# A second block of weights converted behind the attention's first stage, and half of the next layer's weights inside that layer's loop

## The chip, the cores and the metric

The kernel runs on one core of a Trainium2 chip. The metric is the device time of one execution in microseconds (us), the median of several runs. Five engines matter: PE (TensorE, the matrix multiplier), DVE (VectorE), ACT (ScalarE), POOL (GpSimd) and SP (SyncE, which here only issues DMA transfers). Each works through its own list of instructions in the order in which the program puts them there.

## The reference

Three stages follow one another: a causal attention with a bias from a running sum, a feed-forward layer with a PReLU, and one with a gate by a clipped sum. Cut to what matters:

```python
# attention: 4 batches x 8 heads x 576 positions x 64
scores = q @ k.T / sqrt(64)
cum = cumsum(maximum(s, 0))
scores = where(causal, -1e6 or lower, scores + minimum(-(cum_row - cum_col), 0))
attn = exp(scores - max); attn = attn / (sum(attn) + 1e-9)
x = attn @ v                                   # 2304 tokens x 512
# layer one: 512 -> 2048 -> 512
h = x @ w_in;  g = maximum(h, 0) + alpha * minimum(h, 0);  y = g @ w_out
# layer two: 512 -> 2048 -> 512
h = y @ w_in2; g = h * clip(h + 3, 0, 6) / 6;              out = g @ w_out2
```

The weights come as 64-bit floats.

## The kernel before, in words

**Precision.** Every product of the two layers is three matmuls: each operand is split into a high and a low part of a 32-bit type (`fp32r`), and high by low, low by high and high by high are added up. A matmul works on a 128x128 weight and up to 512 columns.

**Weights.** A layer's weights are read as pairs of 32-bit words and converted on the chip. They come in eight units; a unit serves two of the sixteen steps `f` of the layer's hidden dimension. `load_unit` issues its four transfers on SP (tiles `wraw`, 512 KB each), and `split_unit` converts it in two parts, each with one tile of the first matrix (`wi`) and one of the second (`wo`). `split_part` (L128 to L159) is one part: ACT takes the upper words over into a buffer `wcv` (L141, per tile), POOL clamps that (L143) and writes a copy back (L146), ACT prepares the lower words of `wi` (L149; only outside the attention's first stage), DVE puts the words together (L151, and L154 where L149 did not run), ACT rounds to the high part (L157) and DVE subtracts for the low part (L158). So a unit is 10 instructions on DVE outside the first stage and 12 for a unit whose buffers belong to it, 8 on POOL, and 8 to 10 on ACT. `wi` of both parts is needed for step `f`'s first product, since a part is half of the contraction.

**Stages.** The first stage (L633 to L636) is the attention of the first 256 tokens of each batch for the heads of batches 0 and 1 (eight pairs of heads): scores (PE L242), bias and maximum on DVE (L234, L247), a mask on POOL (L236), exponentials on ACT (L251), scaling on POOL (L255), transposes on PE (L486) and values (L493, L494), whose result ACT and DVE split into `xhi` (L498) and `xlo` (L499). The second stage (L637 to L672) runs layer one for those tokens (blocks 0 and 1, 512 columns at a time) with the heads of batch 2 and more between its steps. `moe1` (L544) is layer one: step `f` makes `h` (PE, helper `products`, L181; 12 matmuls), `gt` on ACT and DVE (L581, L582), `gh` (ACT L585) and `gl` (DVE or POOL, L586), and some steps later the second product `y` (PE L559; 12 matmuls). After the second stage come the rest of the attention with layer one for blocks 3 and on, then a last call of layer one for the last two blocks (L698 to L704), which also converts the second weights (`more_w2`), and layer two (L710 to L762): `h` (PE L749), `gt` (ACT L751, DVE L752), `gh` and `gl` (ACT L755, DVE L756) and `o` (PE L722, L725), with the next block's input fetched at step 4 (`load_y`, L688: a transfer, ACT L694, DVE L695).

**What sets the order.** The program's own scheduler orders each engine's list by priorities; `tc.high_priority(offset=...)` shifts them. `more_w` converts the first weights' next unit: inside the first stage with the offset `WP0`, which puts the work behind other work; `W_AT` names the heads at which `attend` calls it there. `tc.keep_in_program_order` ties an instruction to a place behind the one that the program wrote before it on the same engine. Conversion buffers `wcv` lie in the stage's pool (`Pools`), six of them in the first stage; a later stage's buffers take the same memory and wait until it is free.

Of the kernel before, what the change touches and what calls it, by code (L numbers as in the profile page):

```python
# [22 lines left out]
WB0 = 6  # L23
WB = 4

W_LD = (8, 11, 14)
W_AT = (2, 14)

A2_AT = 2
A2_OF = 11  # L30
# [10 lines left out]
W_SCALE = 2.0**-112  # L41
W_MOST = struct.unpack("f", struct.pack("I", 0x0FEFFFFF))[0]
# [16 lines left out]
def attention_moe_moe(ctx, tc, qt, kt, qn, kn, vp, s, w_in1, w_out1, alpha, w_in2, w_out2, out):  # L59

    nc = tc.nc
# [8 lines left out]
    NU = 8  # L70
# [22 lines left out]
    def bank(role):  # L93
        turn[role] = turn.get(role, -1) + 1
        i = roles[role][turn[role] % len(roles[role])]
        return ps.tile([P, 512], F32, tag=f"b{i}", name=role)
# [28 lines left out]
                raw[nm, part] = t  # L125
        return j, raw

    def split_part(unit, part, pool, tag, bufs):  # L128
        j, raw = unit
        names = [("wi", part), ("wo", part)]  # L130
        ops = []
        for key in names:
            c = pool.tile([P, CH], U32, tag=tag, bufs=bufs, name="wcv")
            r = raw[key]
            half = r.bitcast(U16).rearrange("p f (t b) -> p f t b", t=2)

            beside = (half[:, :, 1, 0], half[:, :, 0, 1]) if bufs != WB0 and key[0] == "wi" else None
            ops.append((c, c.bitcast(F32), r[:, :, 1], r[:, :, 0], beside))

        for c, cf, high, low, beside in ops:  # L140
            nc.scalar.activation(cf, high.bitcast(F32), AF.Copy, scale=W_SCALE)  # L141
        for c, cf, high, low, beside in ops:
            nc.gpsimd.tensor_scalar(cf, cf, W_MOST, -W_MOST, op0=ALU.min, op1=ALU.max)  # L143

        for c, cf, high, low, beside in ops:
            nc.gpsimd.tensor_scalar(high.bitcast(F32), cf, 0.0, 1.0, op0=ALU.mult, op1=ALU.mult)  # L146
        for c, cf, high, low, beside in ops:
            if beside:
                nc.scalar.activation(*beside, AF.Copy, scale=1.0 / 8192, bias=-4095.5 / 8192)  # L149
        for c, cf, high, low, beside in ops:  # L150
            nc.vector.scalar_tensor_tensor(c, c, 3, high, op0=ALU.logical_shift_left, op1=ALU.bitwise_or)  # L151
        for c, cf, high, low, beside in ops:
            if not beside:
                nc.vector.scalar_tensor_tensor(c, low, 29, c, op0=ALU.logical_shift_right, op1=ALU.bitwise_or)  # L154
        for key, (c, cf, *_) in zip(names, ops):
            t = wp.tile([P, 2, CH], F32R, tag=f"{key[0]}{j}{part}", name=key[0])
            nc.scalar.activation(t[:, 0, :], cf, AF.Copy)  # L157
            nc.vector.tensor_tensor(t[:, 1, :], cf, t[:, 0, :].bitcast(F32), op=ALU.subtract)  # L158
            raw[key] = t  # L159

    def split_unit(unit, pool, tag, bufs):
        for part in range(NP):
            split_part(unit, part, pool, tag, bufs)
        return unit[1]

    def w_in_of(w, kc, f):
# [428 lines left out]
    units, w1, units2, w2 = [], [], [], []  # L595

    def load_w1(n):
        while len(units) < n:
            units.append(load_unit(w_in1, w_out1, len(units)))

    def more_w(pool):
        if len(w1) < NU:
            load_w1(len(w1) + 1)
            with tc.high_priority(offset=WP0 if pool.wb == WB0 else 0):
                w1.append(split_unit(units[len(w1)], pool, "wcv", pool.wb))

    def more_w2(f, pool):

        if f >= 2 and f % 2 == 0 and len(units2) < NU:
            units2.append(load_unit(w_in2, w_out2, len(units2)))  # L610
        if f >= 6 and f % 2 == 0 and len(w2) < NU:
            with tc.high_priority(offset=W2P):
                w2.append(split_unit(units2[len(w2)], pool, "wcv", pool.wb))

# [59 lines left out]
    with ExitStack() as st:  # L674
        pool = Pools(st, tc, "attb", ("kraw qraw vraw ks qh ql vs cum", "t", "xf pth ptl"))
# [22 lines left out]
    with ExitStack() as st:  # L698
        pool = Pools(st, tc, "last", ("g5 gh5 gl5 wcv",), WB)
# [10 lines left out]
    with ExitStack() as ph2:  # L710
        m2 = Pools(ph2, tc, "moe2", ("y", "g gh gl ot", "wcv"))
# [86 lines left out]
```

## Time and profile before

| | us |
|---|---|
| median of 3 runs | 1040.13 (1039.94 to 1040.81) |
| the profiled execution, whole | 1040.27 |
| its span (first to last instruction) | 1038.5 |
| PE busy | 1012.4 (97%) |
| DVE busy | 622.5 (60%) |
| ACT busy | 567.9 (55%) |
| POOL busy | 432.6 (42%) |

The page of the profile gives each engine's busy time and the chain of work that ended last. The timeline lists instructions in order of time: start and length in us, the engine, the line of the program, the operation, the tiles (output, arrow, inputs), and how many equal ones were merged; in brackets stands how long the engine was idle ahead of it and what released it. Starts count from the beginning of the span. The view by stretches gives for each stretch the busy time of every engine, the clock that PE was granted as a share of its upper level of 2.4 GHz, and the load of the DMA engines. The view by lines groups instructions.

### The profile page before, as it was taken

The numbers are of one execution on the slowest core, as the hardware profiler recorded it, in microseconds if no ns is written. First come the engines' busy times: TensorE is split into PE (matmuls) and PEld (weight loads), VectorE is DVE, ScalarE is ACT, GpSimd is POOL, SyncE is SP. The second block draws the span as 40 slices with busy tenths as digits, with TensorE's granted clock in tenths as the row PEclk, the third lists the DMA queues.
The fourth block names the chain that finished last, engine by engine and source line by source line (L and its number), as shares of the span: only waits on it lengthen the run. The fifth ranks groups of instructions, "written<-read, shape, count | busy, mean of one in ns | idle before, by whom it ended". The sixth has DMA issues, their size and how long they took to land.

```text
span 1038.5 us, 17002 instructions
## 1 busy us (share of the span) xinstructions
PE 1012.4 (97%) x5843; PEld 868.1 (84%) x5843; DVE 622.5 (60%) x1520; ACT 567.9 (55%) x1286; POOL 432.6 (42%) x625
## 2 busy tenths in 40 slices
PE   7899999999999999999999998999999999999998
PEld 3457777999999999999998886888888888888897
DVE  4849995668888888888854999623222322222222
ACT  3557885767776767777745788523222422322232
POOL 4836763957877778877731664200000000000000
PEclk6799999999999999999999999999999999999999
DMA  6829004413334233334206653100100100000010
GB/s 205 307 75 351 12 16 116 144 46 110 94 92 122 82 98 111 100 97 113 69 8 209 238 187 132 66 1 9 73 1 1 61 1 0 21 21 1 1 41 21
DMA packets 55893, 89.59 MB, mean 86 GB/s; under 512 B 5568, under 2 KB 29888, under 8 KB 55808
## 3 DMA queue, kind: packets, MB, share of 16 engines
q1 hardware_dynamic: 55808, 88.52, 27.2%
q8 instruction: 46, 0.75, 0.3%
q14 instruction: 39, 0.32, 0.1%
HBM read 78.99 MB, written 9.51 MB: 85 GB/s over the span
## 4 chain that ended last, share of the span: by engine, by line
PE 88%; DVE 3%; ACT 3%; DMA 2%; issue 1%; POOL 1%; SPq 1%; ACTq 0%; POOLq 0%; DVEq 0%
PE h L749 18%; PE h L181 18%; PE y L559 18%; PE o L722 13%; PE o L725 6%; PE s L319 4%; PE pv L381 4%; PE pt L356 4%; PE s L242 1%; DMA wraw<-in_w_in 1%; PE pt L486 1%; PE pv L493 1%; ACT wcv L141 1%; ACT t L251 0%; DVE wcv L154 0%
## 5 line engine op out<-in xcount | busy, mean ns | idle before, releaser
L181 PE MATMUL h<-xhi,wi 128*128 128x256 f32 (+1 forms) x896 | 221.2, 317 | 1.6 <-DVE gt L582 1.5
L749 PE MATMUL h<-yhl,wi 128*128 128x512 f32 (+1 forms) x960 | 213.6, 371 | 4.1 <-DVE gt L752 4.1
L749 PEld LDWEIGHTS h<-yhl,wi 128*128 128x128 f32 x960 | 170.4, 189 | 37.6 <-DVE gt L752 4.5
L752 DVE SCALAR_TENSOR_TENSOR gt<-gt,h 128x512 f32<-128x512 f32 (+1 forms) x80 | 50.6, 634 | 211.6 <-ACT gt L751 211.3
L181 PEld LDWEIGHTS h<-xhi,wi 128*128 128x128 f32 x896 | 154.6, 189 | 15.7 <-DVE gt L582 2.6
L559 PE MATMUL y<-gh,wo 128*128 128x256 f32 (+1 forms) x896 | 162.3, 316 | 0.0
L751 ACT ACTIVATE gt<-h,three 128x512 f32<-128x512 f32 (+1 forms) x80 | 51.4, 645 | 200.4 <-PE h L749 199.6
L722 PE MATMUL o<-wo,gh 128*128 128x512 f32 x576 | 145.7, 391 | 0.1
L559 PEld LDWEIGHTS y<-gh,wo 128*128 128x128 f32 x896 | 132.7, 190 | 11.6 <-issue 1.3
L181 PE MATMUL h<-xlo,wi 128*128 128x256 f32 (+1 forms) x448 | 141.4, 316 | 0.0
L722 PEld LDWEIGHTS o<-wo,gh 128*128 128x128 f32 x576 | 106.8, 188 | 22.7 <-ACT gh L755 0.6
L559 PE MATMUL y<-gl,wo 128*128 128x256 f32 (+1 forms) x448 | 93.8, 317 | 0.0
L181 PEld LDWEIGHTS h<-xlo,wi 128*128 128x128 f32 x448 | 84.8, 189 | 6.0 <-issue 0.2
L327 ACT ACTIVATE t<-t,m 128x384 f32<-128x384 f32 (+2 forms) x96 | 67.5, 703 | 40.6 <-DVE m L322 39.5
L143 POOL TENSOR_SCALAR wcv<-wcv 128x512 f32<-128x512 f32 x64 | 52.0, 817 | 88.1 <-ACT wcv L141 85.0
L756 DVE TENSOR_TENSOR gl<-gt,gh 128x512 fp32r<-128x512 f32 (+1 forms) x80 | 51.2, 641 | 55.5 <-ACT gh L755 45.8
L331 POOL TENSOR_SCALAR t<-t,rec 128x384 f32<-128x384 f32 (+2 forms) x96 | 67.6, 705 | 30.7 <-DVE rec L330 22.3
L725 PE MATMUL o<-wo,gl 128*128 128x512 f32 x288 | 79.4, 390 | 0.0
L755 ACT ACTIVATE gh<-gt 128x512 fp32r<-128x512 f32 (+1 forms) x80 | 47.1, 588 | 56.0 <-DVE gt L752 41.1
L582 DVE SCALAR_TENSOR_TENSOR gt<-gt,beta,h 128x256 f32<-128x256 f32 (+1 forms) x112 | 61.4, 549 | 26.2 <-ACT gt L581 25.5
L559 PEld LDWEIGHTS y<-gl,wo 128*128 128x128 f32 x448 | 70.8, 190 | 5.9 <-issue 0.3
L586 POOL TENSOR_TENSOR gl<-gt,gh 128x256 fp32r<-128x256 f32 x80 | 63.1, 788 | 29.8 <-ACT gh L585 29.7
(101 smaller groups left out, 1787.4 us busy)
## 6 DMA issues: line engine op xcount, KB each, us to landing
wraw<-in_w_in SPq DMA_DIRECT2D x32, 512.0 KB, 5.4
wraw<-in_w_out SPq DMA_DIRECT2D x32, 512.0 KB, 5.7
kraw<-in_kt SPq DMA_DIRECT2D x32, 288.0 KB, 2.8
cumk<-cum_scratch SPq DMA_DIRECT2D x32, 288.0 KB, 3.3
qraw<-in_qt SPq DMA_DIRECT2D x32, 160.0 KB, 2.7
vraw<-in_vp SPq DMA_DIRECT2D x32, 160.0 KB, 2.2
y_scratch<-yt SPq DMA_DIRECT2D x18, 256.0 KB, 3.0
yr<-y_scratch SPq DMA_DIRECT2D x4, 1024.0 KB, 5.2
```

The lines of the kernel that those rows point to most:

```text
L143: nc.gpsimd.tensor_scalar(cf, cf, W_MOST, -W_MOST, op0=ALU.min, op1=ALU.max)
L181: nc.tensor.matmul(dst, lt, r, start=first and i == 0, stop=last and i == len(terms) - 1)
L327: nc.scalar.activation(t[:n, :w], t[:n, :w], AF.Exp, bias=m[-1][:n], scale=-1.0, accum_out=den[:n])
L331: nc.gpsimd.tensor_scalar(t[:n, :w], t[:n, :w], rec[:n], 1.0, op0=ALU.mult, op1=ALU.mult)
L559: nc.tensor.matmul(ys[dc // per][:, o : o + n], which[:, dc * P : (dc + 1) * P], gg, start=(f == 0 and which is wl and dc % per == 0), sto ...
L582: nc.vector.scalar_tensor_tensor(gt, gt, beta[:, f : f + 1], hp[:, :n], op0=ALU.mult, op1=ALU.add)
L586: (nc.vector if n == 512 else nc.gpsimd).tensor_tensor(gl, gt, gh.bitcast(F32), op=ALU.subtract)
L722: nc.tensor.matmul(op[i], lt[:, tsl], r, start=(f == 0 and r is wh), stop=False)
L725: nc.tensor.matmul(op[i], gl[:, tsl], wh, start=False, stop=(f == FC - 1))
L749: nc.tensor.matmul(hp[:, :n], lt, r, start=(i == 0), stop=(i == len(terms) - 1))
L751: nc.scalar.activation(gt[:, :n], hp[:, :n], AF.Relu, bias=three)
L756: nc.vector.tensor_tensor(gl[:, :n], gt[:, :n], gh[:, :n].bitcast(F32), op=ALU.subtract)
```

## The change

Four edits:

- `W_AT` goes from (2, 14) to (2, 17): the first weights' second unit (unit 1, for steps 2 and 3) is converted when the program's loop over the first stage's heads is over, not at head 14. Its instructions get the new `pin`, by which each keeps its place behind the instruction that the program wrote before it on its engine.
- The first stage's pools are set up in another order, so that the conversion buffers `wcv` lie last.
- `more_w2` stops at four units (`NU // 2`) in place of eight. Before, six units were written in that last call of layer one, and two more in layer two's loop.
- Layer two's loop writes the other four units (4 to 7), with `pin`, at its steps 4, 6, 8 and 10 of the first block.

```diff
-W_AT = (2, 14)
+W_AT = (2, 17)
...
-    def split_part(unit, part, pool, tag, bufs):
+    def split_part(unit, part, pool, tag, bufs, pin=False):
+        keep = tc.keep_in_program_order if pin else (lambda ins: ins)
...
-            nc.scalar.activation(cf, high.bitcast(F32), AF.Copy, scale=W_SCALE)
+            keep(nc.scalar.activation(cf, high.bitcast(F32), AF.Copy, scale=W_SCALE))
...
-                w1.append(split_unit(units[len(w1)], pool, "wcv", pool.wb))
+                w1.append(split_unit(units[len(w1)], pool, "wcv", pool.wb, pin=len(w1) == 1))
...
-        if f >= 6 and f % 2 == 0 and len(w2) < NU:
+        if f >= 6 and f % 2 == 0 and len(w2) < NU // 2:
...
-        pool = Pools(st, tc, "att0", ("wcv", "kraw qraw vraw cum", "t pT"), WB0)
+        pool = Pools(st, tc, "att0", ("kraw qraw vraw cum", "t pT", "wcv"), WB0)
...
-                    w2.append(split_unit(units2[len(w2)], m2, "wcv", 3))
+                    w2.append(split_unit(units2[len(w2)], m2, "wcv", 3, pin=True))
```

`keep` goes around each of the eight instructions of `split_part` in the same way. Lines from 129 on stand two lower in the kernel after (L149 is L151 there, L582 is L584).

The names in the rows below: `h_886` and `h_942` belong to steps 0 and 1, `h_1082` and `h_1118` to steps 2 and 3, `h_1220` to step 4; `wcv_802`, `803`, `820`, `821` with `wi_814`, `wo_817`, `wi_832`, `wo_835` are unit 1 in the kernel after; `wcv_850` to `869` are unit 2 and `906` to `925` unit 3; `t_982` and `s_988` are the second stage's first head.

DVE, at the end of the first stage, before: behind the last `xlo` come the gates of steps 0 and 1, between them the bias of the second stage's first heads, and unit 2's conversion.

```order
L499 TENSOR_TENSOR xlo_82<-pv_831,xhi_81 128x256
L582 SCALAR_TENSOR_TENSOR gt_899<-gt_899,beta_79,h_886 128x512
L234 TENSOR_SCALAR t_982<-cumk_969,cq_83 128x128
L234 TENSOR_SCALAR t_982<-cumk_969,cq_83 128x256
L582 SCALAR_TENSOR_TENSOR gt_955<-gt_955,beta_79,h_942 128x512
L234 TENSOR_SCALAR t_1002<-cumk_969,cq_83 128x128
L234 TENSOR_SCALAR t_1002<-cumk_969,cq_83 128x256
L586 TENSOR_TENSOR gl_903<-gt_899,gh_902 128x512
L586 TENSOR_TENSOR gl_959<-gt_955,gh_958 128x512
...
L151 SCALAR_TENSOR_TENSOR wcv_850<-wcv_850,wraw_597 128x512
L151 SCALAR_TENSOR_TENSOR wcv_851<-wcv_851,wraw_599 128x512
```

After, the same place: the gates, then the conversion of units 2, 1 and 3, 32 instructions (`wcv_850` to `wo_835`), of which the sixteenth is unit 1's `wi_814` and the last two are `wi_832` and `wo_835`; only then step 2's gate and the first head.

```order
L501 TENSOR_TENSOR xlo_82<-pv_795,xhi_81 128x256
L584 SCALAR_TENSOR_TENSOR gt_899<-gt_899,beta_79,h_886 128x512
L584 SCALAR_TENSOR_TENSOR gt_955<-gt_955,beta_79,h_942 128x512
L588 TENSOR_TENSOR gl_903<-gt_899,gh_902 128x512
L588 TENSOR_TENSOR gl_959<-gt_955,gh_958 128x512
L153 SCALAR_TENSOR_TENSOR wcv_850<-wcv_850,wraw_597 128x512
...
L160 TENSOR_TENSOR wi_814<-wcv_802,wi_814 128x512
...
L160 TENSOR_TENSOR wo_939<-wcv_925,wo_939 128x512
L160 TENSOR_TENSOR wi_832<-wcv_820,wi_832 128x512
L160 TENSOR_TENSOR wo_835<-wcv_821,wo_835 128x512
L584 SCALAR_TENSOR_TENSOR gt_1095<-gt_1095,beta_79,h_1082 128x512
L236 TENSOR_SCALAR t_982<-cumk_969,cq_83 128x128
```

The conversion of three units has moved ahead of the second stage's first head, in one piece.

PE, at the same place, before: the last matmuls of steps 0 and 1, the scores of the first head, and the matmuls of step 2, whose weights (`wi_733`, `wi_751`, unit 1 of that kernel) were converted in the first stage.

```order
L181 MATMUL h_886<-xhi_81,wi_251 128x512
L181 MATMUL h_942<-xlo_82,wi_251 128x512
L181 MATMUL h_942<-xhi_81,wi_251 128x512
L242 MATMUL s_988<-kraw_962,qraw_964 128x128
L242 MATMUL s_988<-kraw_962,qraw_964 128x256
L181 MATMUL h_1082<-xhi_81,wi_733 128x512
L181 MATMUL h_1082<-xlo_82,wi_733 128x512
L181 MATMUL h_1082<-xhi_81,wi_733 128x512 x2
L181 MATMUL h_1082<-xlo_82,wi_733 128x512
L181 MATMUL h_1082<-xhi_81,wi_733 128x512
L181 MATMUL h_1082<-xhi_81,wi_751 128x512
L181 MATMUL h_1082<-xlo_82,wi_751 128x512
```

After: behind steps 0 and 1 come their second products `y` (24 matmuls, of which the last stands first here), 12 matmuls of steps 2 and 3 on `wi_814`, 12 on `wi_832`, and then the first head's scores and step 4 on unit 2 (`wi_862`).

```order
L561 MATMUL y_1105<-gl_959,wo_254 128x512
L183 MATMUL h_1082<-xhi_81,wi_814 128x512
...
L183 MATMUL h_1118<-xhi_81,wi_814 128x512
L183 MATMUL h_1082<-xhi_81,wi_832 128x512
L183 MATMUL h_1082<-xlo_82,wi_832 128x512
...
L183 MATMUL h_1118<-xhi_81,wi_832 128x512
L244 MATMUL s_988<-kraw_962,qraw_964 128x128
L244 MATMUL s_988<-kraw_962,qraw_964 128x256
L183 MATMUL h_1220<-xhi_81,wi_862 128x512
L183 MATMUL h_1220<-xlo_82,wi_862 128x512
```

The scores of the second stage's first head have moved from behind 24 matmuls of layer one to behind 72.

DVE, at the start of layer two, before: conversion stands right ahead of the first two gates of layer two (`gt2`).

```order
L154 SCALAR_TENSOR_TENSOR wcv_9324<-wraw_9095,wcv_9324 128x512
L154 SCALAR_TENSOR_TENSOR wcv_9631<-wraw_9203,wcv_9631 128x512
L158 TENSOR_TENSOR wi_9642<-wcv_9630,wi_9642 128x512
L158 TENSOR_TENSOR wo_9338<-wcv_9324,wo_9338 128x512
L158 TENSOR_TENSOR wo_9645<-wcv_9631,wo_9645 128x512
L752 SCALAR_TENSOR_TENSOR gt2_9366<-gt2_9366,h_9353 128x512
L752 SCALAR_TENSOR_TENSOR gt2_9386<-gt2_9386,h_9373 128x512
```

After: the last call of layer one's gates stand there, and the first conversion (`wcv_9401`, unit 4) comes behind the gates of four more steps.

```order
L584 SCALAR_TENSOR_TENSOR gt_9218<-gt_9218,beta_79,h_9205 128x512
L588 TENSOR_TENSOR gl_9222<-gt_9218,gh_9221 128x512
L754 SCALAR_TENSOR_TENSOR gt2_9294<-gt2_9294,h_9281 128x512
L697 TENSOR_TENSOR yhl_9471<-yr_9469,yhl_9471 128x512 x4
...
L754 SCALAR_TENSOR_TENSOR gt2_9450<-gt2_9450,h_9437 128x512
L758 TENSOR_TENSOR gl2_9454<-gt2_9450,gh2_9453 128x512
L153 SCALAR_TENSOR_TENSOR wcv_9401<-wcv_9401,wraw_8981 128x512
L153 SCALAR_TENSOR_TENSOR wcv_9402<-wcv_9402,wraw_8983 128x512
L156 SCALAR_TENSOR_TENSOR wcv_9402<-wraw_8983,wcv_9402 128x512
L160 TENSOR_TENSOR wi_9413<-wcv_9401,wi_9413 128x512
```

The conversions ahead of layer two's first gates have gone, and four units now stand between its steps.

## Rows read from the trace of the kernel before

**Rows 1.** The page, busy time by engine.

```profile
PE 1012.4 (97%) x5843; PEld 868.1 (84%) x5843; DVE 622.5 (60%) x1520; ACT 567.9 (55%) x1286; POOL 432.6 (42%) x625
```

**Rows 2.** Timeline of ACT, DVE and PE around the end of stage one.

```profile
73.72 0.39 ACT L498 ACTIVATE xhi<-pv 128x256 fp32r<-128x256 f32 x1 [4.46 <-PE pv L494]
74.00 2.32 ACT L141 ACTIVATE wcv<-wraw 128x512 f32<-128x512 f32 x4
76.22 1.07 ACT L581 ACTIVATE gt<-h 128x512 f32<-128x512 f32 x2
77.62 0.63 ACT L585 ACTIVATE gh<-gt 128x512 fp32r<-128x512 f32 x1 [0.33 <-DVE gt L582]
...
79.57 1.49 DVE L586 TENSOR_TENSOR gl<-gt,gh 128x512 fp32r<-128x512 f32 x2
...
88.66 0.61 PE L559 MATMUL y<-gh,wo 128*128 128x512 f32 x2
```

**Rows 3.** View by lines, 74 to 160 us: busy, mean ns of one, idle before.

```profile
L151 DVE SCALAR_TENSOR_TENSOR wcv<-wcv,wraw 128x512 uint32<-128x512 uint32 x24 | 18.5, 778 | 3.0 <-ACT wraw L149 2.8
L158 DVE TENSOR_TENSOR wi<-wcv,wi 128x512 fp32r<-128x512 f32 x12 | 11.0, 919 | 0.7 <-ACT wi L157 0.7
L158 DVE TENSOR_TENSOR wo<-wcv,wo 128x512 fp32r<-128x512 f32 x12 | 9.9, 828 | 1.6 <-ACT wo L157 1.4
L154 DVE SCALAR_TENSOR_TENSOR wcv<-wraw,wcv 128x512 uint32<-128x512 uint32 x12 | 9.5, 793 | 0.0
...
L149 ACT ACTIVATE wraw<-wraw 128x512 uint16<-128x512 uint16 x12 | 16.3, 1357 | 0.0
L141 ACT ACTIVATE wcv<-wraw 128x512 f32<-128x512 f32 x24 | 15.9, 675 | 3.3 <-DVE wi L158 1.7 <-DVE wo L158 1.5
...
L157 ACT ACTIVATE wi<-wcv 128x512 fp32r<-128x512 f32 x12 | 7.6, 634 | 1.4 <-DVE wcv L151 1.4
```

**Rows 4.** Timeline of DVE ahead of layer two's first gates.

```profile
638.16 1.28 DVE L151 SCALAR_TENSOR_TENSOR wcv<-wcv,wraw 128x512 uint32<-128x512 uint32 x2
...
646.30 1.28 DVE L752 SCALAR_TENSOR_TENSOR gt<-gt,h 128x512 f32<-128x512 f32 x2
```

**Rows 5.** Stretches: length, busy of PE, PEld, DVE, ACT, POOL; PE clock, DMA.

```profile
156.00:182.00 26.00, 25.08 (x141) 20.84 (x140) 14.49 (x38) 13.93 (x37) 10.26 (x17) 1.00 0.41 118
182.00:208.00 26.00, 24.40 (x199) 23.54 (x198) 16.70 (x58) 19.82 (x65) 25.11 (x41) 1.00 0.47 141
...
638.00:646.00 8.00, 4.98 (x22) 3.76 (x20) 7.90 (x14) 7.37 (x13) 0.00 (x0) 1.00 0.49 160
```

**Rows 6.** PE at layer two's start (timeline); twelve matmuls at full clock (chain).

```profile
647.03 7.36 PE L749 MATMUL h<-yhl,wi 128*128 128x512 f32 x24 [4.05 <-DVE gt L752]
...
99.53 2.72 PE y L559 x12
```

**Rows 7.** Issues on SP (timeline); landing of weight loads, 70 to 130 us.

```profile
73.75 0.80 SPq L476 DMA_DIRECT2D cumk<-cum_scratch  x2
...
77.44 0.43 SPq L123 DMA_DIRECT2D wraw<-in_w_in  x1
...
DMA to landing us min/median/max: 7.0/9.3/10.5
```

**Rows 8.** Stage one: PE (timeline), clock (stretches), unit 1's first DVE step.

```profile
35.74 0.92 PE L242 MATMUL s<-kraw,qraw 64*128 64x128 f32 x4 [1.58 <-DVE m L247]
38.68 1.65 PE L242 MATMUL s<-kraw,qraw 64*128 64x128 f32 x4 [2.02 <-DVE m L247]
...
60.57 1.15 PE L486 MATMUL pt<-ident,t 128*128 128x128 f32 x3 [1.17 <-POOL t L255]
...
48.00:50.00 2.00, 1.92 (x6) 1.20 (x7) 2.00 (x5) 0.66 (x2) 2.00 (x3) 0.50 0.71 252
...
62.00:64.00 2.00, 2.00 (x8) 1.08 (x7) 0.00 (x1) 0.80 (x2) 2.00 (x6) 0.50 0.00 0
...
44.63 0.68 DVE L151 SCALAR_TENSOR_TENSOR wcv<-wcv,wraw 128x512 uint32<-128x512 uint32 x1
```

More of the change, by code (lines that the diff above doesn't have):

```diff
@@ L140, in split_part, with split_unit @@
         for c, cf, high, low, beside in ops:
-            nc.scalar.activation(cf, high.bitcast(F32), AF.Copy, scale=W_SCALE)
+            keep(nc.scalar.activation(cf, high.bitcast(F32), AF.Copy, scale=W_SCALE))
         for c, cf, high, low, beside in ops:
-            nc.gpsimd.tensor_scalar(cf, cf, W_MOST, -W_MOST, op0=ALU.min, op1=ALU.max)
+            keep(nc.gpsimd.tensor_scalar(cf, cf, W_MOST, -W_MOST, op0=ALU.min, op1=ALU.max))
         for c, cf, high, low, beside in ops:
-            nc.gpsimd.tensor_scalar(high.bitcast(F32), cf, 0.0, 1.0, op0=ALU.mult, op1=ALU.mult)
+            keep(nc.gpsimd.tensor_scalar(high.bitcast(F32), cf, 0.0, 1.0, op0=ALU.mult, op1=ALU.mult))
         for c, cf, high, low, beside in ops:
             if beside:
-                nc.scalar.activation(*beside, AF.Copy, scale=1.0 / 8192, bias=-4095.5 / 8192)
+                keep(nc.scalar.activation(*beside, AF.Copy, scale=1.0 / 8192, bias=-4095.5 / 8192))
         for c, cf, high, low, beside in ops:
-            nc.vector.scalar_tensor_tensor(c, c, 3, high, op0=ALU.logical_shift_left, op1=ALU.bitwise_or)
+            keep(nc.vector.scalar_tensor_tensor(c, c, 3, high, op0=ALU.logical_shift_left, op1=ALU.bitwise_or))
         for c, cf, high, low, beside in ops:
             if not beside:
-                nc.vector.scalar_tensor_tensor(c, low, 29, c, op0=ALU.logical_shift_right, op1=ALU.bitwise_or)
+                keep(nc.vector.scalar_tensor_tensor(c, low, 29, c, op0=ALU.logical_shift_right, op1=ALU.bitwise_or))
         for key, (c, cf, *_) in zip(names, ops):
             t = wp.tile([P, 2, CH], F32R, tag=f"{key[0]}{j}{part}", name=key[0])
-            nc.scalar.activation(t[:, 0, :], cf, AF.Copy)
-            nc.vector.tensor_tensor(t[:, 1, :], cf, t[:, 0, :].bitcast(F32), op=ALU.subtract)
+            keep(nc.scalar.activation(t[:, 0, :], cf, AF.Copy))
+            keep(nc.vector.tensor_tensor(t[:, 1, :], cf, t[:, 0, :].bitcast(F32), op=ALU.subtract))
             raw[key] = t
-    def split_unit(unit, pool, tag, bufs):
+    def split_unit(unit, pool, tag, bufs, pin=False):
         for part in range(NP):
-            split_part(unit, part, pool, tag, bufs)
+            split_part(unit, part, pool, tag, bufs, pin)
         return unit[1]
```

## The prediction

> **What bounds the kernel now.** The page's busy times come first: PE works 1012.4 of 1038.5 us [rows 1], so the kernel is PE's list of matmuls and a change pays only where PE waits or runs at a lower clock. The timeline of PE and the view by stretches then show where that is: in the first stage, 0 to 78 us; a little at 156 to 208 us, where 0.92 and 1.60 us of two stretches of 26 us are idle [rows 5]; and 4.05 us ahead of 647.03, where layer two waits for its first gates on DVE [rows 6]. Between 78 and 156 us nothing is to be had on PE, but DVE is busy there with the conversion of units 2 to 7: the 60 instructions of the view by lines [rows 3]. So the question is what each edit does to DVE's list at these places, since DVE takes its list strictly in order.
>
> **Part one: unit 1 behind the last head.** What it removes from stage one are 12 DVE, 8 POOL and 8 ACT instructions, of which the first on DVE stands at 44.63 [rows 8]. What it adds stands in the order of DVE: units 1, 2 and 3 come in one piece of 32 instructions between `gl` of step 1 and the gate of step 2. I count from the last `xhi` (73.72 before [rows 2]) and call that time zero.
>
> ACT first takes six `wcv` in place of four; at 2.32/4 = 0.58 us each that is 0.3 + 3.5 = 3.8, two `gt` of 1.07 end at 4.9 [rows 2], DVE's two gates at about 5.6, the second `gh` at 6.2, and the two `gl` of 1.49 leave DVE free at 7.1. PE has finished `h` of steps 0 and 1 by then and does the 24 `y` matmuls, to about 11.2 (2 x 2.72 from 5.7 [rows 6]). Then it has nothing: the next 12 matmuls want `wi_814`, the sixteenth of the 32, the following 12 want `wi_832`, the thirty-first, and the second stage's first head comes behind those on PE and behind all 32 on DVE. Nothing else is in PE's list there, so nothing covers this wait.
>
> How long do 31 conversions take on DVE? The lower bound is the piece at 638.16 to 646.30, 13 of them in 8.14 us or 0.63 each [rows 4], where POOL did nothing at all [rows 5]: 31 x 0.63 = 19.5. In 74 to 160 us, with POOL converting beside for part of the time, the four rows give 0.78, 0.92, 0.83 and 0.79 us [rows 3]; over the mix of the 31 that is 25.4. With waits for ACT's `L149` and `L157` (3.0 + 0.7 + 1.6 us for 60 instructions [rows 3], so 2.8 for 31) it is 28.2. POOL has 24 conversions right there, of which some nine are done by 7.1, so DVE is beside a working POOL until about two thirds of the piece and alone after it; I take 26.7, nearer to the upper end. So `wi_832` is ready at 33.8 (26.6 to 35.3). ACT's own share, 12 L141, 12 L157, four L149 and four gate steps, is 12 x 0.675 + 12 x 0.634 + 4 x 1.357 + 2.4 = 23.5 us [rows 2, 3], less than DVE's, so DVE sets the end.
>
> PE then does its last 12 of these 72 matmuls. After the 4.05 us wait at 647.03, 24 matmuls took 7.36 us where 24 at full clock take 5.44 [rows 6], so a wait of this kind costs 1.9 us more: 33.8 + 2.7 + 1.9 = 38.4. Before, the same 72 matmuls (steps 0 to 3 of `h`, 0 and 1 of `y`) were done at 88.66 [rows 2], which is 14.9. **The loss is 23.5 us**, with 17 (no lost clock, the fast pace) to 29 (every conversion at 0.9, waits of 3 us, two clock losses) as bounds.
>
> A rule bears on the pace. The Trainium skill, page "SBUF — State Buffer", section "Who interferes with whom", has it that a DVE instruction with two SBUF inputs and a GpSimd instruction that reads SBUF exclude each other for the whole instruction, while the rows show only a stretch from 0.63 to 0.83 on average. What a full exclusion would give is a rival below.
>
> **What it moves on SP.** With the pools in their new order the first buffers of pair 8 (`vraw`, `cumk`) lie where unit 1's `wcv` were and wait for `wi_832` and `wo_835`. Behind them on SP's list wait the other pairs' loads and the raw weights of units 4 to 7. Before, `cumk` was issued at 73.75 and the first raw tile at 77.44, 3.7 us behind it, landing 7.0 to 10.5 us later [rows 7]. So unit 4's first tile lands at about 34.5 + 3.7 + 9.3 = 47.5, and ACT's list has its first step behind the `gh` of step 4, which comes at about 44. ACT then stands for some 3 us with gates behind it; PE has other steps of `h` and `y` in between. I take +2 (0 to 6).
>
> **What stage one gives back.** On DVE the 12 instructions cost about 12 x 0.65 = 8 us, beginning at 44.63; yet PE has its full work there at half clock, which held until about 50 [rows 8], and its waits of 1.58 and 2.02 us stand ahead of 44.63. What is left to gain is the wait of 1.17 at 60.57 for POOL and the half clock behind it (62 to 64: 0.50 [rows 8]; some 3.6 us, so 1.8 lost): 3.0 in all. I take −3, between +1 (heads collide on other engines) and −7 (also a half of the loss at half clock up to 50).
>
> **What comes back later.** The conversions of units 2 and 3 no longer compete with the heads, so the 2.5 us that PE waits in 156 to 208 us [rows 5] can shrink: −2 (−2.5 to 0).
>
> **Part two: four units of the second weights.** Ahead of layer two's first gates the conversions are gone from DVE's list. The wait of 4.05 and the clock behind it, 1.9 [rows 6], go: −5.9. What is late next is the last `gh` and `yt` of layer one on ACT, which PE's remaining `y` and `h` of steps 0 to 2 cover. The four units come between layer two's steps instead. One unit costs ACT 4 x 0.675 + 2 x 1.357 + 4 x 0.634 = 8.0 us [rows 3] within two steps of PE, which are 4 x 2.72 = 10.9 us [rows 6], beside 2.5 us for its own gates; so ACT is full, and as the conversion is pinned, a step that waits for DVE holds the gates behind it. PE runs its `h` about one step ahead, which covers the first 5.4 us of it. I take +1.5 (0 to 8).
>
> **The sum.** 23.5 + 2 − 3 − 2 − 5.9 + 1.5 = +16.1. On the profiled execution's 1040.27 us this is 1056.4; the median lay 0.14 us under that execution, so 1056.2, and I say **1056**.
>
> **The rivals.**
>
> First, DVE and POOL exclude each other fully. For: all conversions take longer beside POOL [rows 3, 4]. Against: the mean is 0.83 and not 1.26. POOL's 15 remaining instructions of at least 0.63 would add 9.5 to 19.5, so `wi_832` comes at 36.2, 2.4 later than in the sum: **1059**. (This is the page's rule, named above.)
>
> Second, **faster**: stage one is held up by unit 1 everywhere, through its POOL and ACT instructions too, and without it loses neither the waits of 1.58, 2.02 and 1.17 us nor the clock (about 12 us at half level to 50, so 6, and 1.8 behind 60.57 [rows 8]): 12.6 us less. With the start's loss at its lower bound of 17.5, 0 on SP, −2 and −5.9 it comes to 1040.3 − 3.0 = **1037**. It decides at the last `xhi`: it must stand at 61 us or earlier. Against: these waits end on DVE's `m` 6 to 9 us ahead of unit 1's first DVE instruction [rows 8].
>
> Third, **no change**: each term at its favourable end, start 17, stage one −7, later −2.5, boundary −5.9: **1042** or a little less. It decides at the pace, 0.63 against 0.83.
>
> Fourth, slower by more: pinned conversions stall PE at each of the eight parts by 1 us, and unit 4 comes 6 us late: 1056 + 6.5 + 4 = **1067**. For it speaks ACT's budget of 10.5 in 10.9 us.
>
> That the change does not do what it says is excluded by the order of the lists.
>
> **How the numbers follow.** I give the forecast 0.66, full exclusion 0.13, faster 0.08, no change 0.05, and slower by more 0.08. What a measurement of this kernel can tell from no change is 0.2%, some 2 us. So faster is 0.08, same 0.05, slower 0.87. The forecast's own terms, added at their ends, would reach from 1042 to 1070; for 8 in 10 I take 1041 to 1068, which leaves out the faster case and half of the fourth.
>
> **What would show it.** In the profile after, `wi_832` (DVE, the line that makes the low part) should end 33 us behind the last `xhi`, and PE should show two waits of 8 to 10 us there that name DVE or ACT conversions, with a lower clock behind each. The first scores of the second stage should stand 38 us behind the last `xhi`, where before it was 2.4. The last `xhi` should stand at 70 to 71. Layer two's start should show no wait over 1 us for a gate and full clock. Wrong it would be if PE found the weights of steps 2 and 3 ready, if the last `xhi` came before 65, or if layer two's first block showed waits of more than 2 us in all.

## The result, and the profile after

The changed kernel took 1054.94 us (median of 4, 1053.73 to 1055.18) beside 1040.47 us of the kernel before on the same chip: a ratio of 1.0135, with a 95% interval of 1.0118 to 1.0153. Forecast were 1056 us and 1041 to 1068. The profiled execution has a span of 1053.0 us, 14.5 more than before.

The page of the kernel after, busy time by engine, beside [rows 1]:

```profile
PE 1013.3 (96%) x5843; PEld 867.3 (82%) x5843; DVE 617.7 (59%) x1520; ACT 569.2 (54%) x1286; POOL 429.9 (41%) x625
```

PE has the same work as before (1013.3 against 1012.4 us), and so all of the loss but 0.9 us is time in which it waits. The view by stretches (length, then busy time of PE, PEld, DVE, ACT and POOL, PE's clock, DMA) shows where:

```profile
52.00:78.00 26.00, 22.75 (x111) 15.14 (x110) 10.39 (x32) 14.74 (x35) 12.05 (x21) 1.00 0.07 20
78.00:104.00 26.00, 7.17 (x22) 5.18 (x21) 23.20 (x30) 13.60 (x20) 12.18 (x13) 0.65 0.01 3
...
156.00:182.00 26.00, 26.00 (x127) 20.80 (x124) 18.86 (x30) 16.11 (x31) 9.28 (x10) 1.00 0.01 2
182.00:208.00 26.00, 24.86 (x166) 22.20 (x166) 14.06 (x45) 16.21 (x49) 15.84 (x27) 1.00 0.59 179
208.00:312.00 104.00, 101.72 (x815) 98.18 (x814) 77.84 (x238) 72.34 (x200) 80.71 (x121) 1.00 0.29 86
...
600.00:650.00 50.00, 50.00 (x222) 41.38 (x221) 36.29 (x50) 30.21 (x46) 19.29 (x20) 1.00 0.57 179
```

From 78 to 104 us PE is busy for 7.17 of 26 us and DVE for 23.20. The 0.92 us of 156 to 182 [rows 5] are gone, but 1.14 and 2.28 us stand in the two stretches behind, and at 600 to 650, where layer two begins, nothing is idle.

The timeline around the end of stage one, in the order ACT, PE and DVE, beside [rows 2] (start, length, what ran; in brackets the idle time ahead of it and what released it):

```profile
67.80 0.39 ACT L500 ACTIVATE xhi<-pv 128x256 fp32r<-128x256 f32 x1 [4.80 <-PE pv L496]
68.08 3.43 ACT L143 ACTIVATE wcv<-wraw 128x512 f32<-128x512 f32 x6
71.41 1.08 ACT L583 ACTIVATE gt<-h 128x512 f32<-128x512 f32 x2
...
73.50 2.12 PE L561 MATMUL y<-gh,wo 128*128 128x512 f32 x8 [3.25 <-ACT gh L587]
89.49 0.80 PE L183 MATMUL h<-xhi,wi 128*128 128x512 f32 x1 [10.25 <-DVE wi L160]
102.48 0.80 PE L183 MATMUL h<-xhi,wi 128*128 128x512 f32 x1 [8.58 <-DVE wi L160]
107.11 0.92 PE L244 MATMUL s<-kraw,qraw 64*128 64x128 f32 x4
...
87.31 1.12 DVE L153 SCALAR_TENSOR_TENSOR wcv<-wcv,wraw 128x512 uint32<-128x512 uint32 x1
88.35 1.09 DVE L160 TENSOR_TENSOR wi<-wcv,wi 128x512 fp32r<-128x512 f32 x1
92.43 1.11 DVE L156 SCALAR_TENSOR_TENSOR wcv<-wraw,wcv 128x512 uint32<-128x512 uint32 x1
99.34 0.68 DVE L153 SCALAR_TENSOR_TENSOR wcv<-wcv,wraw 128x512 uint32<-128x512 uint32 x1
101.75 0.68 DVE L160 TENSOR_TENSOR wi<-wcv,wi 128x512 fp32r<-128x512 f32 x1
```

The last `xhi` stands at 67.80, 5.9 us earlier than before. Then PE waits 3.25 us for the first gate, 10.25 for `wi_814` and 8.58 for `wi_832`, which ends at 102.43, 34.6 us behind the last `xhi`. The 72 matmuls of layer one that were done 14.9 us behind it before are done at 107.11, 39.3 behind it; only there do the first scores of the second stage stand. DVE's steps take 1.02 us from start to start while POOL converts beside it (five from 87.31 to 92.43) and 0.60 once it does not (the last four).

At layer two's start the kernel after has this on PE, beside [rows 6]:

```profile
655.43 9.11 PE L751 MATMUL h<-yhl,wi 128*128 128x512 f32 x39
```

39 matmuls in a row at 0.23 us each, with no idle time ahead of them, where 24 took 7.36 us behind a wait of 4.05 us before.

So the 14.5 us are: +24.4 at the start (39.3 − 14.9), +0.9 for the first head's four score matmuls, which before lay inside the 72, −5.9 by stage one, −5.9 at layer two's start (4.05 and 1.9 of clock), and +0.3 by PE's waits at 156 to 400 us (3.4 against 3.1). That is 13.8; the other 0.7 were not traced to a place.

### The profile page after: what moved, and what is told of

The parts are those of the page before. It is cut to its first block, busy times and chain, and to the rows that moved or that the text cites. A ratio compares the mean times of both kernels' runs of the same rounds, so it can differ in the third digit from the quotient of the medians.

```text
span 1053.0 us, 16998 instructions
## 1 busy us (share of the span) xinstructions
PE 1013.3 (96%) x5843; PEld 867.3 (82%) x5843; DVE 617.7 (59%) x1520; ACT 569.2 (54%) x1286; POOL 429.9 (41%) x625
## 4 chain that ended last, share of the span: by engine, by line
PE 88%; DVE 4%; DMA 3%; ACT 2%; POOL 1%; issue 1%; SPq 1%; ACTq 0%; POOLq 0%; DVEq 0%
PE h L751 19%; PE h L183 18%; PE y L561 17%; PE o L724 12%; PE o L727 6%; PE s L321 4%; PE pv L383 4%; PE pt L358 3%; PE s L244 1%; DVE wcv L153 1%; DMA cumk<-cum_scratch 1%; PE h L446 1%; PE pv L495 1%; PE pt L488 1%; DMA wraw<-in_w_out 1%
## 5 line engine op out<-in xcount | busy, mean ns | idle before, releaser
L183 PE MATMUL h<-xhi,wi 128*128 128x256 f32 (+1 forms) x896 | 222.9, 320 | 20.0 <-DVE wi L160 18.8
L584 DVE SCALAR_TENSOR_TENSOR gt<-gt,beta,h 128x256 f32<-128x256 f32 (+1 forms) x112 | 61.3, 549 | 41.1 <-ACT gt L583 40.1
L583 ACT ACTIVATE gt<-h 128x256 f32<-128x256 f32 (+1 forms) x112 | 49.3, 441 | 44.0 <-PE h L183 41.0
```

What stands on the lines that cost most here:

```text
L183: nc.tensor.matmul(dst, lt, r, start=first and i == 0, stop=last and i == len(terms) - 1)
L584: nc.vector.scalar_tensor_tensor(gt, gt, beta[:, f : f + 1], hp[:, :n], op0=ALU.mult, op1=ALU.add)
```

## The experiments

The theory was that of the forecast: the two parts of the change add up; the first loses by shutting PE's next work behind one piece of conversions on DVE, the second gains the boundary. The rivals stand with each run. All times are medians of four or five runs; the ratio to the kernel before, run beside them, has its 95% interval.

### Each part alone

The second weights' part alone keeps `W_AT`, the pools and unit 1 as before:

```diff
-W_AT = (2, 17)
+W_AT = (2, 14)
...
-                w1.append(split_unit(units[len(w1)], pool, "wcv", pool.wb, pin=len(w1) == 1))
+                w1.append(split_unit(units[len(w1)], pool, "wcv", pool.wb))
...
-        pool = Pools(st, tc, "att0", ("kraw qraw vraw cum", "t pT", "wcv"), WB0)
+        pool = Pools(st, tc, "att0", ("wcv", "kraw qraw vraw cum", "t pT"), WB0)
```

> Only the edits on the second weights (four units ahead of layer two, four pinned between its steps); the first weights and the pools as before. Theory (the start loses, layer two's start gains 4.05 us of wait and 1.9 us of clock): 1040.4 - 5.9 = 1034.5 us, no PE wait over 1 us at layer two's start and none in its first block. Rival (the gain at the boundary in the changed kernel came only because its early part ran later): 1039 to 1041 us with a wait of about 4 us left.

Measured: 1035.15 us, ratio 0.9943 (0.9926 to 0.9960), faster than both kernels, and PE is busy for all of 600 to 650 us, where layer two begins. The first weights' part alone undoes the other two lines:

```diff
-        if f >= 6 and f % 2 == 0 and len(w2) < NU // 2:
+        if f >= 6 and f % 2 == 0 and len(w2) < NU:
...
-                    w2.append(split_unit(units2[len(w2)], m2, "wcv", 3, pin=True))
+                    w2.append(split_unit(units2[len(w2)], m2, "wcv", 3))
```

> Only the edits on the first weights and the pools; the second weights as before. Theory (the two parts add up): 1054.9 + 5.9 = 1060.8 us, PE waits of 3, 10 and 9 us behind the first stage as in the changed kernel, and a wait of about 4 us at layer two's start. Rival (the early delay moves the loads so that the boundary stall hides): 1055 us.

Measured: 1061.57 us, 1.0200 (1.0185 to 1.0215). The parts add up: −5.4 and +21.0 make +15.6, and both together gave +14.5. In its timeline the boundary's wait is back:

```profile
667.19 8.21 PE L751 MATMUL h<-yhl,wi 128*128 128x512 f32 x24 [4.36 <-DVE gt L754]
```

4.36 us of waiting for the gate and 24 matmuls in 8.21 us; without both, as in the changed kernel, 6.6 us less.

### What shuts PE's work away: the pin, and the pools' order

Two runs undo one line each of the first part. The first puts the pools back into the order of before:

```diff
-        pool = Pools(st, tc, "att0", ("kraw qraw vraw cum", "t pT", "wcv"), WB0)
+        pool = Pools(st, tc, "att0", ("wcv", "kraw qraw vraw cum", "t pT"), WB0)
```

> The changed kernel with the first stage's pools in the order of before; unit 1 still pinned behind the last head. The second stage's heads no longer wait for unit 1's buffers, and on DVE's list their bias stands ahead of the conversions. Theory A (the loss is that the heads are shut behind the conversions, so PE has nothing else): most of the 20 us of waits go, 1038 to 1044 us. Theory B (the loss is unit 1's place alone: the matmuls of steps 2 and 3 want it, wherever the heads stand): the waits stay at 15 us or more, 1050 to 1055 us.

Measured: 1043.57 us, 1.0034 (1.0021 to 1.0047), 11.4 less than the changed kernel, for one line that changes no instruction. Its timelines of SP and PE and its stretches, beside SP's issues in the changed kernel:

```profile
102.45 0.80 SPq L462 DMA_DIRECT2D vraw<-in_vp  x2
103.35 0.86 SPq L478 DMA_DIRECT2D cumk<-cum_scratch  x2
```

```profile
71.96 0.92 PE L244 MATMUL s<-kraw,qraw 64*128 64x128 f32 x4 [1.29 <-DVE m L249]
75.29 1.64 PE L244 MATMUL s<-kraw,qraw 64*128 64x128 f32 x4 [2.41 <-DVE m L249]
81.47 1.65 PE L244 MATMUL s<-kraw,qraw 64*128 64x128 f32 x4 [1.07 <-DVE m L249]
92.32 0.80 PE L183 MATMUL h<-xhi,wi 128*128 128x512 f32 x1 [1.34 <-DVE gt L584]
...
78.00:104.00 26.00, 22.86 (x81) 15.47 (x82) 21.96 (x62) 19.46 (x49) 18.77 (x32) 0.66 0.84 311
156.00:182.00 26.00, 22.81 (x108) 18.10 (x107) 22.82 (x51) 16.15 (x41) 19.43 (x29) 1.00 0.39 101
```

The first of these stretches in e1 reads

```profile
78.00:104.00 26.00, 25.50 (x112) 19.72 (x113) 23.62 (x55) 19.02 (x38) 16.75 (x25) 1.00 1.00 356
```

In the changed kernel `vraw` and `cumk` of the second stage's first pair are issued at 102.45 and 103.35, when `wi_832` and `wo_835` have set unit 1's buffers free. With the pools in the old order the scores of the first heads run at 71.96 to 81.47, and the longest wait of PE there is 2.4 us. Theory A holds, at the upper end of its range. The scores' own loads were not late in the changed kernel either: `kraw` and `qraw` of that pair were issued at 65.00 and 65.43. So it is the place of the scores in PE's list that the pools' order moves; that the scheduler puts them back because `vraw` and `cumk` come late is inferred from SP's issues and not shown. What is left over e1 is 8.4 us, though the last `xhi` stands 7.2 us earlier (67.36 against 74.58): at 78 to 104 us PE is busy for 22.86 of 26 us, but at a clock of 0.66, so that it does 81 matmuls where e1 does 112, and at 156 to 182 us it misses 3.2 us.

The second run leaves everything but the pin:

```diff
-                w1.append(split_unit(units[len(w1)], pool, "wcv", pool.wb, pin=len(w1) == 1))
+                w1.append(split_unit(units[len(w1)], pool, "wcv", pool.wb))
```

> The changed kernel with unit 1 written behind the last head but not pinned: on DVE's list it goes back between the heads of stage one. Pools in the new order. Theory (the pin is what makes it late; the pools' order costs nothing by itself): as before less the 5.9 us at layer two's start, 1034 to 1036 us, first stage's last xhi back at about 73 us. Rival (the pools' new order delays the second stage's loads whatever the place of unit 1): 1040 us or more, with a wait on a transfer behind the first stage.

Measured: 1034.28 us, 0.9936 (0.9922 to 0.9951); last `xhi` at 72.82. Without the pin the scheduler takes unit 1 back between stage one's heads, in spite of where the program writes it, and the pools' order costs nothing. So neither line alone is the loss: the pin puts unit 1 behind the last head (20.7 us over e4 with the new pools, 8.4 over e1 with the old), and the pools' order then makes the next stage's loads wait for it and puts that stage's heads behind it.

### The place within the piece

```diff
-            with tc.high_priority(offset=WP0 if pool.wb == WB0 else 0):
+            with tc.high_priority(offset=WP0 if pool.wb == WB0 and not w1 else 0):
```

> The changed kernel with the shift WP0 taken off unit 1, so that on DVE's list wi_832 is the 21st conversion and not the 31st; unit 3 comes behind the first head. Theory (PE waits for the place of wi_832 in the piece, at about 0.85 us a conversion): 8.5 us less, 1046 to 1047 us, wi_832 about 26 us behind the last xhi. Rival (the heads' late loads on SP set the pace, so the place within the piece does not count): 1053 us or more, with a wait on a transfer in the place of the one on DVE.

Measured: 1068.43 us, 1.0263 (1.0243 to 1.0283). The time lies in the rival's range but without its sign, since PE's wait still names DVE and not a transfer. The start did what the theory said; the rest did not:

```profile
93.42 0.79 PE L183 MATMUL h<-xhi,wi 128*128 128x512 f32 x1 [9.37 <-DVE wi L160]
...
78.00:104.00 26.00, 16.17 (x63) 12.16 (x62) 21.42 (x36) 16.11 (x27) 15.58 (x15) 0.80 0.28 68
182.00:208.00 26.00, 22.03 (x159) 20.97 (x158) 10.06 (x27) 14.24 (x41) 17.31 (x26) 0.87 0.73 210
208.00:312.00 104.00, 99.55 (x801) 96.28 (x800) 75.45 (x233) 69.19 (x197) 74.52 (x115) 1.00 0.24 74
312.00:400.00 88.00, 84.98 (x655) 80.12 (x654) 73.75 (x223) 61.94 (x169) 67.06 (x99) 0.98 0.35 103
400.00:600.00 200.00, 196.07 (x1454) 184.26 (x1453) 154.88 (x435) 132.34 (x348) 126.71 (x184) 0.99 0.32 99
```

`wi_832` comes 25.6 us behind the last `xhi` (26 expected), and PE is idle for 9.8 us at 78 to 104 where it was for 18.8. But from 182 to 600 us PE is idle for 15.4 us where the changed kernel has 3.4, and its clock is 0.87, 0.98 and 0.99 in three of these stretches. The program's scheduler had put PE's list into another order: in the traces it differs from that of the changed kernel from 114 us of that kernel on to 634 us, so this run does not hold the rest still. Which change of that order costs the 15 us was not found.

### DVE beside POOL

A run without POOL's clamp in these three units was to show how much of DVE's pace is POOL's doing:

```diff
-        for c, cf, high, low, beside in ops:
+        for c, cf, high, low, beside in ops if clamp else []:
             keep(nc.gpsimd.tensor_scalar(cf, cf, W_MOST, -W_MOST, op0=ALU.min, op1=ALU.max))
...
-                w1.append(split_unit(units[len(w1)], pool, "wcv", pool.wb, pin=len(w1) == 1))
+                w1.append(split_unit(units[len(w1)], pool, "wcv", pool.wb, pin=len(w1) == 1, clamp=len(w1) not in (1, 2, 3)))
```

> The changed kernel without POOL's clamp (12 instructions) in units 1, 2 and 3 of the first weights: that part of the conversion is left out. Theory (DVE's pace of 0.68 without and 1.02 to 1.09 us with POOL beside it is contention between the two): with 12 of 24 POOL instructions gone wi_832 comes 3 to 5 us earlier, 1050 to 1052 us, and the DVE steps that are left beside POOL still take about 1.0 us. Rival (the pace is set by waits for ACT's steps): 1054 to 1055 us.

Measured: 1060.35 us, 1.0189 (1.0173 to 1.0205): slower by 5.4 than the changed kernel. Here too the order of PE's list was another, from 78 to 634 us of the changed kernel, so it decides nothing. It was repeated with half the clamp, a size at which PE's and SP's lists stay as they are and the other lists differ only within the piece:

```diff
-            keep(nc.gpsimd.tensor_scalar(cf, cf, W_MOST, -W_MOST, op0=ALU.min, op1=ALU.max))
+            keep(nc.gpsimd.tensor_scalar(*[cf if clamp else cf[:, :256]] * 2, W_MOST, -W_MOST, op0=ALU.min, op1=ALU.max))
```

> The changed kernel with POOL's clamp in units 1, 2 and 3 cut to the first 256 of 512 columns (the other half of these weights is not clamped). On PE and SP the order of instructions is that of the changed kernel from the first row to the last; on DVE, ACT and POOL it differs only inside the piece of conversions behind stage one. So e6 is repeated without a new order later on. Theory (DVE shares a port with POOL, and e6 was slower only by its new order from 180 us on): 12 x 0.3 us of POOL's time goes, wi_832 comes 1.5 to 3.5 us earlier, 1051.5 to 1053.5 us, and nothing changes from 110 us on. Rival (less work on POOL does not help DVE, and e6 shows it): 1055 us or more.

Measured: 1051.44 us, 1.0105 (1.0088 to 1.0122), 3.5 less than the changed kernel. From its timelines of PE, DVE and POOL, and two lines each from the views by lines of DVE's piece, first the changed kernel's:

```profile
86.87 0.80 PE L183 MATMUL h<-xhi,wi 128*128 128x512 f32 x1 [6.39 <-DVE wi L160]
97.47 0.80 PE L183 MATMUL h<-xhi,wi 128*128 128x512 f32 x1 [5.55 <-DVE wi L160]
...
96.73 0.68 DVE L160 TENSOR_TENSOR wi<-wcv,wi 128x512 fp32r<-128x512 f32 x1
...
85.88 0.40 POOL L145 TENSOR_SCALAR wcv<-wcv 128x256 f32<-128x256 f32 x1 [0.44 <-ACT wcv L143]
...
L156 DVE SCALAR_TENSOR_TENSOR wcv<-wraw,wcv 128x512 uint32<-128x512 uint32 x8 | 6.6, 840 | 0.0
L160 DVE TENSOR_TENSOR wi<-wcv,wi 128x512 fp32r<-128x512 f32 x6 | 4.9, 821 | 1.4 <-ACT wi L159 1.4
...
L156 DVE SCALAR_TENSOR_TENSOR wcv<-wraw,wcv 128x512 uint32<-128x512 uint32 x8 | 5.8, 730 | 0.0
L160 DVE TENSOR_TENSOR wi<-wcv,wi 128x512 fp32r<-128x512 f32 x6 | 5.6, 941 | 0.0
```

`wi_832` ends 30.7 us behind the last `xhi`, 4.0 earlier (1.5 to 3.5 expected), and PE's two waits are 6.39 and 5.55 us. One half clamp alone takes 0.40 us, so twelve of them take some 2.5 us off POOL's list. But only a part of the 4.0 us is faster DVE steps: over all lines of the piece the 32 conversions are busy for 25.7 us where they were for 26.7, and the 2.5 us in which DVE waited for ACT's steps in the changed kernel are all but gone, with ACT's steps in another order. So less work on POOL goes with about 1 us on DVE, and whether the rest comes from it or from the new order is not shown. The contention itself shows in the changed kernel's steps of 1.02 and 0.60 us above: at 0.68 us each, the length of a step with POOL at rest, 32 conversions would be busy for 21.8 us, so by this estimate about 4.9 of the 26.7 us are steps drawn out beside POOL. How hard the two engines hold each other up, a piece of e5's POOL and DVE timelines shows:

```profile
81.58 5.87 POOL L145 TENSOR_SCALAR wcv<-wcv 128x512 f32<-128x512 f32 x2 [3.53 <-ACT wcv L143]
...
80.91 0.68 DVE L153 SCALAR_TENSOR_TENSOR wcv<-wcv,wraw 128x512 uint32<-128x512 uint32 x1
83.92 0.68 DVE L160 TENSOR_TENSOR wi<-wcv,wi 128x512 fp32r<-128x512 f32 x1
85.72 0.68 DVE L160 TENSOR_TENSOR wo<-wcv,wo 128x512 fp32r<-128x512 f32 x1
```

Two clamps took 5.87 us, which alone take 1.2, while DVE ran its conversions at 0.60 from start to start without a break, from 80.3 to 86.4; the first of the two took 5.30 us, the second, behind that piece, 0.61. So POOL can be shut out for some 4.7 us as well as slow DVE down. The Trainium skill, page "SBUF — State Buffer", section "Who interferes with whom", has it that the pair of ports that DVE and GpSimd share is an exclusive lock, and that the order of issue decides who is blocked: the trace agrees for POOL in this piece. Where both run in turns the trace does not show the full sum: one step of each takes 1.02 us together (87.31 to 92.43 in the kernel after, five steps) and not 0.60 + 0.61.

### What the pin does in layer two

```diff
-                    w2.append(split_unit(units2[len(w2)], m2, "wcv", 3, pin=True))
+                    w2.append(split_unit(units2[len(w2)], m2, "wcv", 3))
```

> Only four units ahead of layer two, the other four between its steps but not pinned. Theory (the gain at layer two's start comes from what is written ahead of it, the pin only keeps the scheduler from pulling units 4 to 7 forward): with the scheduler free some conversions come back ahead of the first gates and a part of the wait returns, 1035 to 1039 us. Rival (the pin does nothing): 1035 us as with it, no wait at layer two's start.

Measured: 1032.90 us, 0.9927 (0.9912 to 0.9942), and no PE wait at layer two's start: the rival's sign, at a time below both ranges. The same was tried on e4; its edit is that of e4 and the one above together:

> As e4 (W_AT 17 and new pools, unit 1 not pinned), and the second weights' units 4 to 7 not pinned either, as in e7. Theory (the pins have no worth of their own, and the number of units ahead of layer two does it all): 1033 to 1034 us, no wait at layer two's start. Rival (e7's lead of 2 us over e1 came from the missing pin): 1032 us or less.

Measured: 1034.02 us, 0.9938 (0.9923 to 0.9953), as the theory had it. e1, e4, e7 and e10 are 1032.9 to 1035.2 us with intervals that overlap, so the pin in layer two has no worth that these runs can tell; that four units and not six stand ahead of layer two is what gains. e7, the kernel before with `NU // 2` as its one edit, is the simplest of the four, and faster than both kernels.

### What unit 1 costs in stage one, and whether another place is cheaper

```diff
-                w1.append(split_unit(units[len(w1)], pool, "wcv", pool.wb, pin=len(w1) == 1))
+                w1.append(w1[0] if len(w1) == 1 else split_unit(units[len(w1)], pool, "wcv", pool.wb))
```

> The changed kernel without any conversion of unit 1: steps 2 and 3 of layer one use unit 0's weights, so the output is another; the transfers stay. Theory (unit 1 in stage one costs PE the 6 us by which the last xhi came earlier in the changed kernel, and nothing takes them back later): last xhi at 67 to 68 us, 1028 to 1029 us. Rival (what stage one gives is taken back by waits at 130 to 310 us, since the heads come as slowly as before): 1032 to 1035 us.

Measured: 1028.51 us, last `xhi` at 67.06: 5.8 us less than e4 (1034.28, 72.82), and the 5.8 us of stage one are kept to the end. So moving unit 1 elsewhere can hardly gain more than that. Two other places for it were tried, with the pools in the old order and no pins:

```diff
-W_AT = (2, 17)
+W_AT = (2,)
```

> Unit 1 is not converted in stage one at all but as the first unit of stage two's own list, in that stage's buffers; pools in the old order, no pins; second weights four and four. On DVE the bias of five of the second stage's heads and both gates stand ahead of it, and PE has the first scores and 24 y matmuls before it wants unit 1. Theory (the loss came from shutting heads and gates behind one piece of conversions): last xhi at 67 us, PE waits 3 to 6 us for unit 1, 1031 to 1035 us. Rival (unit 1 behind the last head costs its 12 conversions in any order, some 10 to 13 us with the clock): 1039 us or more.

Measured: 1046.84 us, 1.0061 (1.0046 to 1.0076), last `xhi` at 69.46: the rival, and not by one wait. Its stretches:

```profile
78.00:104.00 26.00, 24.05 (x106) 17.45 (x104) 24.17 (x66) 20.32 (x49) 19.03 (x28) 0.93 0.88 332
104.00:130.00 26.00, 23.94 (x106) 18.03 (x105) 21.49 (x43) 21.68 (x41) 17.13 (x22) 0.93 0.06 16
130.00:156.00 26.00, 22.67 (x108) 17.36 (x108) 24.08 (x40) 18.91 (x35) 19.01 (x25) 0.99 0.27 72
156.00:182.00 26.00, 21.46 (x88) 17.23 (x87) 18.59 (x45) 17.74 (x47) 18.44 (x25) 0.82 0.16 46
```

PE misses 1.95, 2.06, 3.33 and 4.54 us in the four stretches, 11.9 in all where the kernel before misses 0.9, and its clock falls to 0.93, 0.93, 0.99 and 0.82. Of these waits 10.3 us name DVE: 5.1 a gate, 3.9 a `wi`, 1.3 a head's maximum. In the kernel before, the first of the four reads

```profile
78.00:104.00 26.00, 26.00 (x117) 20.18 (x116) 23.62 (x54) 19.32 (x38) 16.97 (x25) 1.00 0.97 350
```

and the next two have 24.4 and 23.6 us of DVE as well: with the conversions of [rows 3] in it DVE has 6.4 us left in these three stretches, less than the 8 us that unit 1 takes. The last run splits unit 1, its first part in stage one and its second in stage two:

```diff
-W_AT = (2,)
+W_AT = (2, 14)
...
     def more_w(pool):
+        if pool.wb == WB0 and len(w1) == 1:
+            load_w1(2)
+            with tc.high_priority(offset=WP0):
+                split_part(units[1], 0, pool, "wcv", pool.wb)
+            half.append(1)
+            return
+        if half:
+            half.pop()
+            split_part(units[1], 1, pool, "wcv", pool.wb)
+            w1.append(units[1][1])
```

> As e9, but the first of unit 1's two parts is converted in stage one. Theory (stage one is short of DVE and clock, not of room: each part costs it about 3 us): last xhi at 70 us; half the conversions behind it, a PE wait of 0 to 3 us, 1030 to 1034 us. Rival (the stage's clock falls as before with any part in it): last xhi at 72 to 73 us and 1033 to 1036 us.

Measured: 1034.86 us, 0.9942 (0.9926 to 0.9959), last `xhi` at 72.11: the rival's place, and no gain over e1.

## Why the prediction was right

The sign, the two places and the waits at them were those of the forecast, and the sum of 16.1 us met 14.5. That it came so close is in part luck: the terms for stage one, for the later waits, for SP and for the pin were each off by 1.5 to 2.9 us, and not all in one direction. Step by step:

- **The wait behind stage one.** Forecast: `wi_832` 33.8 us behind the last `xhi`, the 72 matmuls done at 38.4, a loss of 23.5. Measured: 34.6, 39.3 and 24.4. The last twelve matmuls took 4.6 us (102.48 to 107.11), as the term for the clock had it (2.7 + 1.9); the profile shows a clock of 0.50 there:

```profile
102.00:104.00 2.00, 1.52 (x4) 1.23 (x5) 1.03 (x2) 0.00 (x0) 0.00 (x0) 0.50 0.14 36
104.00:106.00 2.00, 2.00 (x6) 1.59 (x5) 0.00 (x0) 0.55 (x1) 0.00 (x0) 0.50 0.75 118
```

- **The pace on DVE.** 26.7 us for 31 conversions was taken between two rows. The piece from 75.47 to 102.43 is 26.96 us. The rival of full exclusion (36.2) was not met, but POOL has a part in the pace, by the steps of 1.02 us beside it and 0.60 without.
- **SP, +2.** The loads came late as forecast, and ACT stood 2.62 us for unit 4's first tile; but PE had `h` and `y` of units 2 and 3 in its list and shows no wait from 107 to 198 us. The term was 0.

```profile
117.12 0.67 ACT L143 ACTIVATE wcv<-wraw 128x512 f32<-128x512 f32 x1 [2.62 <-DMA wraw<-in_w_in]
```

- **Stage one, −3.** Mis-sized: it was −5.9, within the bounds given (−7), and the last `xhi` came before the 70 to 71 that were named as a sign. The row that the step rested on was the wait of 1.17 us at 60.57 and the clock behind it [rows 8]; that is gone in the kernel after. But so is the wait of 2.02 us at 38.68, which the step had left out because it stands ahead of unit 1's first DVE instruction (44.63), and half clock lasts from 42 to 48 us in place of 38 to 50. PE's waits of 26 to 68 us are 2.7 us in all, where they were 6.1. Unit 1's work does not begin on DVE: its first POOL clamp stands at 29.91 in the kernel before (first line; the second is PE's largest new wait there in the kernel after). e8 shows that the 5.8 us belong to unit 1. Which of its instructions, on DVE, POOL or ACT, costs them was not tried.

```profile
29.91 0.61 POOL L143 TENSOR_SCALAR wcv<-wcv 128x512 f32<-128x512 f32 x1
...
40.34 0.33 PE L488 MATMUL pt<-ident,t 128*128 128x128 f32 x1 [1.01 <-POOL t L257]
```

- **Later waits, −2.** Wrong in sum: at 156 to 208 us they shrank from 2.5 to 1.1 us, but 2.3 us came up at 208 to 312, so that from 156 to 400 us they are 3.4 where they were 3.1. PE's waits at 198 to 224 us name a gate, an `xf` and a `ptl` of DVE and a `gl` of POOL.
- **Layer two's start, −5.9, and the pin, +1.5.** −5.9 by the trace and −5.4 by e1; the pinned units cost nothing, since no step of the first block waits.
- **The rivals.** Faster was to decide at a last `xhi` of 61 us or earlier; it stood at 67.80. Slower by more needed stalls in layer two; there were none. What the forecast did not name is how much of its 23.5 us belongs to one line: it took the second stage's heads as shut away by the order of the lists, and e3 shows that the pools' order is what puts them there. That edit was told under SP and priced at 2; with the pin in place it is worth 11.4.
- **Two bounds.** They do not follow from the prediction's own terms. With the fast pace and no lost clock the start would lose 7.1 + 19.5 + 2.7 − 14.9 = 14.4 us and not 17 (or 17.5), which puts the third rival at 1039 us; and the terms at their upper ends, the pin's 8 us with them, reach 1078 and not 1070. The sum of 1056 us does not use them; the range does.

## What to carry to other kernels

Work that is moved out of a busy stage has to go where the engine that does it has room, and into a place in that engine's list behind everything that the bottleneck will ask for next. Beside the run that leaves unit 1 out (1028.51 us), its 12 conversions cost about 6 us between the heads (e4), 15 (e3) to 26 us (the changed kernel) in one piece behind them, and 18 us in a stage with DVE at 24 of 26 us (e9). Memory order is a part of the schedule: a buffer that is reused by the next stage makes loads of that stage wait for its last reader, and here one line that sets that order moved the place of the next stage's work in PE's list. And a scheduler that writes the lists anew for each edit makes a single edit a change of the whole rest, so compare the lists of two kernels before you put their times down to the edit.

## What the runs showed of the hardware

- A POOL clamp that takes 0.6 us alone took 5.30 us while DVE ran conversions back to back (e5, from 81.58), so it was held for some 4.7 us, and DVE's conversions went from 0.60 to 1.02 us from start to start beside a working POOL (the changed kernel, 87.31 to 92.43 and 99.94 to 102.35).
- PE's clock was at 0.50, its lower level of 1.2 GHz, from 102 to 106 us behind the wait of 8.58 us. Behind 4.05 and 4.36 us of waiting it was at 0.50 too (649 to 651 us before, 667 to 671 in e2), and 24 matmuls took 7.36 and 8.21 us ([rows 6] and e2). Behind the 3.25 us at 73.50 it was at 1.00, and the 24 `y` matmuls took 5.7 us, close to the 5.4 of the upper level.
